# A scan and expert kernel on one core: the first four resident blocks follow chunk 1 instead of chunk 2

## The chip, the cores and the metric

The kernel runs on one core of one Trainium2 chip. The metric is the device time of one execution in microseconds, as the median of several runs; lower is better. Matmuls run on TensorE (PE; its weight loads are PEld), activations on ScalarE (ACT), elementwise work on VectorE (DVE), indirect DMAs are issued by GpSimd (POOL), and the other DMAs by SyncE (SP).

## What is computed

The reference is a gated linear recurrence over 4 sequences of 3,648 steps and 256 channels, followed by a two-level mixture of 16 experts in which each of the 14,592 tokens goes to one expert:

```python
log_a = c * sig_r * np.log(np.clip(a_base, 1e-06, 1.0 - 1e-06))[None, None, :]
a_t = np.exp(log_a)
x_gated = np.sqrt(np.maximum(1.0 - a_t * a_t, 1e-06)) * sig_i * x
for t in range(S):
    h = a_t[:, t] * h + x_gated[:, t]
    y[:, t] = h
...
g_idx = np.argmax(x @ w_group, axis=1)           # 4 groups, then 4 experts in the group
h = np.maximum(xg[mask_e] @ w1[g, e], 0.0)       # 256 -> 1024
out[tok_idx] = combined[:, None] * (h @ w2[g, e])  # 1024 -> 256, scaled by the two softmax weights
```

## The kernel before, in words

**Chunks.** The tokens are cut into 16 chunks (`SIZES`, in tiles of 128 tokens): chunk 0 has 4 tiles, chunks 1 to 13 have 8, the last two 4 and 2. A chunk's gates are loaded by SP (`load`, L251; tiles `a`, `i`, `x`), made on ACT (L322 to L342) and combined and scanned on DVE (L346, L350, L359). PE then turns the scanned columns into rows, two tiles at a time, with the router's logits beside them (`rows1`, L366; one such call is a row group here and stands as x4 in the order and as x8 in the trace, since the profiler lists two matmuls for each). ACT copies the rows (L372), DVE picks the experts and counts them (L385 to L443; `cn`, L422, is the count), PE ranks the tokens (`rank`, L448 and L449), and POOL writes each row, 276 floats, to its place in its expert's list in DRAM (`scatter`, L469, one DMA for each tile, to the tensor `y_s`). A list has a head of 384 unused rows (`HEAD`), and after the last list lies a region of 256 rows that is cleared at the start (`clear`, L313).

**Resident blocks.** Experts 0, 4, 8 and 12 (`RES`) have their weights loaded at the start (`load_raw`, L968, eight loads of 1,024 KB into w1h0, w1l0 and so on). After the chunks in `RSTAGES` (chunks 2 and 3), and before any other expert work, the kernel takes one block of up to 128 tokens from each of these four lists. `counts` (L598) sums the lists' lengths on PE; `near` (L690) works out on DVE where each block starts, and masks the rows that were taken already; `rows_block` (L1017, L479) reads 128 rows on SP into tiles `hl` and `xl`; `turn_block` (L1026) turns them on PE, ACT copies them (L1030), then come two halves of the first product (L1037), two relus on ACT (L1042) and two halves of the second product (L1049), and the result is scaled and scattered to the output (L1054, L1057). Here R0 is the first set of four blocks and R1 the second.

**Units.** All other tokens go in units of 256 rows: 8, 9 and 9 of them are planned after chunks 4, 7 and 10 (`STAGES`) and 11 after the last chunk, and 16 tails, one for each expert, finish the lists. The first 12 units run in plain float32 (L982, L992, L1006) with weights in the places of the resident experts' weights, unit 0 in that of R0's and R1's block 0; the others run as three products of split operands (L861). A unit's weights can only be loaded when the block before it in the same place is done.

**The order.** Every engine runs its instructions in the order in which they were written. A planner (`Plan`, L43 to L138) decides it: each piece of work is an `op` with an engine, a cost, a due time, what it follows and which ring buffers it takes; `run` advances a clock for each engine and emits, among the pieces that could start soonest, the one with the earliest due time. R0's and R1's pieces are due at their chunk's time plus constants (`add_blocks`, L1063; a chunk has 16.5 in the planner's clock), so the chunk number in `RSTAGES` moves them all.

```python
bs = [Block(s, k, ck.due + ORES + k * STEPB) for k in range(NR)]
...
ga = op("SP", 0.1, lambda m=m: rows_block(m), ck.due + 20, [rows] + scattered, [bg], dma=P * DW * 4)
...
w = temp(tb, NR)
V.scalar_tensor_tensor(w, own, -float(P), dn, op0=ALU.add, op1=ALU.min)
...
V.tensor_tensor(tb.ri, w[0:1], er[0:1], op=ALU.add)
```

The last lines are from `near`: a block starts at min(length - 128, what is done) rows from the list's start. A list with fewer than 128 rows gives a negative start, in the head.

Of the kernel before, what the change touches and what calls it, by code (L numbers as in the profile page):

```python
# [8 lines left out]
F32 = mybir.dt.float32  # L9
# [35 lines left out]
class Plan:  # L45
# [14 lines left out]
    def op(self, engine, cost, emit, due, after=(), new=(), use=(), dma=0, table=None, soon=0.0, order=()):  # L60
        o = Op(engine, cost, emit, due, new, use, dma, table, soon)
        after = dict.fromkeys(a for a in after if a)
        order = dict.fromkeys(a for a in order if a and a not in after)
        o.wait = len(after) + len(order)
        for b in o.new + o.use:
            b.left += 1
        for a in after:
            a.then.append(o)
        for a in order:
            a.next.append(o)  # L70
        self.ops.append(o)
        return o
# [70 lines left out]
def rglru_moe_kernel(ctx: ExitStack, tc: tile.TileContext, x, r_gate, i_gate, a_param,  # L143
                     w_group, w_expert, w1, w2, out):
    nc = tc.nc
    V, S, G, T, DMA = nc.vector, nc.scalar, nc.gpsimd, nc.tensor, nc.sync

    P, NB = 128, 4
# [3 lines left out]
    NE = 16  # L152
# [3 lines left out]
    DW = D + LW  # L156
# [3 lines left out]
    TS = 256  # L160
    BPE = NTOK // TS + 2
    HEAD = 3 * P
# [1 line left out]
    SIZES = [4] + [8] * 13 + [4, 2]   # L164
    CH = 8

    RES, RSTAGES = (0, 4, 8, 12), (2, 3)
    STAGES = [(4, 8), (7, 9), (10, 9)]
    NATIVE = 12

# [1 line left out]
    PBUFS = dict(q_r=2, q_y=1, q_h=2, q_o=1)  # L172
    NA = sum(n for _, n in STAGES)
    NR = len(RES)
    assert NR == 4 and RSTAGES[-1] < STAGES[0][0]

    NP = NT >> 1
    NPS = 37 - NA
# [15 lines left out]
    const = ctx.enter_context(tc.tile_pool(name="const", bufs=1))  # L194
# [4 lines left out]
    rings, pools = {}, {}  # L199
# [13 lines left out]
    y_s = dram.tile([NBLK * TS, DW], F32, name="y_s")  # L213
# [13 lines left out]
    op = plan.op  # L227
# [77 lines left out]
        V.tensor_scalar(tcs[:, k:k + 1], tcol, float(k * P), None, op0=ALU.add)  # L305


    zero = const.tile([P, DW // 2], F32, name="zero")
    V.memset(zero, 0.0)

    def clear(dst):
        k = dst.shape[0] // P
        return DMA.dma_start(dst.rearrange("(p k) (a c) -> p (k a) c", k=k, a=2),  # L313
                             zero.unsqueeze(1).broadcast_to([P, 2 * k, DW // 2]))

    cleared = op("SP", 0.1, lambda: clear(y_s[NE * BPE * TS:, :]), 8.0, dma=5e5, soon=8)

# [1027 lines left out]
```

## Time and profile before

| What | Value |
|---|---|
| median of 3 runs | 957.08 us (954.96 to 960.32) |
| the profiled execution | 946.03 us |
| its span in the profile | 944.3 us |
| PE busy | 856.5 us, 6,082 matmuls |
| DVE, ACT, POOL busy | 620.2, 590.5, 287.0 us |
| DMA | 215.60 MB, mean 228 GB/s |

The profiled execution is one run, and it is 11 us under the median of the others; 1.7 us of its time lie outside the span. In the rows that follow, a line of a timeline gives the start in us, the time from first to last instruction of a merged piece, the engine, the line and the operation, and in brackets the idle time before it and what ended it. The code's line numbers of before are one lower than those of after from L313 on.

### The profile page before, as it was taken

What the parts mean: (1) busy time and instruction counts of PE and PEld (TensorE: products, weight loads), DVE (VectorE), ACT (ScalarE), POOL (GpSimd) and SP (SyncE); (2) the same over time, 40 slices, a digit from 0 to 9 for tenths busy, and PEclk for the clock granted to TensorE, in tenths of its full rate; (3) what the DMA queues carried; (4) which work ended last, traced back from release to release, by engine and by line L of the source; (5) the groups of instructions that cost most, each with busy time, mean ns of one, the idle gap of its engine ahead of it and who ended that gap; (6) DMA issues with size and microseconds to landing.
All of it is one profiled execution on the core that took longest, in us unless ns stands there. A gap on an engine that the chain in (4) does not pass through costs nothing. (4 is left out here: it accounts for less than half of the span.)

```text
span 944.3 us, 18467 instructions
## 1 busy us (share of the span) xinstructions
PE 856.5 (91%) x6082; PEld 821.6 (87%) x6082; DVE 620.2 (66%) x1304; ACT 590.5 (63%) x881; POOL 287.0 (30%) x290
## 2 busy tenths in 40 slices
PE   1335889999999999999999999999999999999984
PEld 1235879988989888999999999999999999999984
DVE  3779777675775426677777777777766666575761
ACT  9999889876797324555555555555645555454541
POOL 2244456465643653111111111111111312122222
PEclk9656889999999999999999999999999999999997
DMA  8997777889886756567667767777763657454410
GB/s 318 424 375 247 278 254 265 297 308 393 292 315 242 232 197 207 159 223 235 214 225 225 229 222 225 225 243 255 234 209 130 189 165 229 136 167 155 131 42 21
DMA packets 72456, 215.60 MB, mean 228 GB/s; under 512 B 10504, under 2 KB 28432, under 8 KB 68241
## 3 DMA queue, kind: packets, MB, share of 16 engines
q1 hardware_dynamic: 60464, 183.04, 58.1%
q0 software_dynamic: 11872, 31.10, 8.6%
q8 instruction: 59, 0.97, 0.4%
q14 instruction: 61, 0.49, 0.1%
HBM read 182.76 MB, written 33.43 MB: 229 GB/s over the span
## 5 line engine op out<-in xcount | busy, mean ns | idle before, releaser
L953 POOL DMA_INDIRECT out_dram<-o,cl x122 | 131.7, 1079 | 484.2 <-ACT o L945 286.1
L469 POOL DMA_INDIRECT y_s<-wf,pi x114 | 135.0, 1184 | 112.8 <-issue 71.4
L865 ACT ACTIVATE a<-q_h 128x384 fp32r<-128x384 f32 (+1 forms) x128 | 56.4, 447 | 108.5 <-PE q_h L861 92.8
L861 PE MATMUL q_h<-x,w1h 128*128 128x384 f32 (+1 forms) x512 | 116.1, 316 | 7.4 <-DVE i L868 6.8
L868 DVE SCALAR_TENSOR_TENSOR i<-q_h,a 128x384 fp32r<-128x384 f32 (+1 forms) x128 | 61.7, 497 | 85.3 <-ACT a L865 81.2
L865 ACT ACTIVATE hh<-q_h 128x512 fp32r<-128x512 f32 x100 | 60.3, 603 | 91.1 <-PE q_h L861 80.8
L861 PE MATMUL q_h<-xh,w1h 128*128 128x256 f32 x400 | 113.2, 283 | 0.0
L861 PE MATMUL q_h<-xl,w1h 128*128 128x256 f32 x400 | 112.6, 282 | 0.0
L861 PE MATMUL q_h<-xh,w1l 128*128 128x256 f32 x400 | 112.4, 281 | 0.0
L816 DVE TENSOR_TENSOR w1l<-wf,w1h 128x1024 fp32r<-128x1024 f32 x82 | 99.9, 1222 | 11.8 <-ACT w1h L814 9.8
L868 DVE SCALAR_TENSOR_TENSOR hl<-q_h,hh 128x512 fp32r<-128x512 f32 x100 | 68.9, 689 | 54.3 <-ACT hh L865 54.2
L366 PE MATMUL q_y<-yw,a 128*128 128x148 f32 x368 | 63.3, 318 | 41.2 <-DVE a L359 32.7
L366 PEld LDWEIGHTS q_y<-yw,a 128*128 128x128 f32 x368 | 57.5, 211 | 47.8 <-DVE a L359 18.8
L816 DVE TENSOR_TENSOR w2l<-wf,w2h 128x1024 fp32r<-128x1024 f32 x82 | 98.2, 1219 | 0.0
L861 PEld LDWEIGHTS q_h<-x,w1h 128*128 128x128 f32 x512 | 84.2, 188 | 9.0 <-issue 6.3
L814 ACT CAST w1h<-wf 128x1024 fp32r<-128x1024 f32 x82 | 86.9, 1064 | 0.3 <-issue 0.3
L814 ACT CAST w2h<-wf 128x1024 fp32r<-128x1024 f32 x82 | 83.9, 1043 | 0.0
L861 PE MATMUL q_h<-x,w1l 128*128 128x384 f32 (+1 forms) x256 | 79.7, 311 | 0.0
L861 PEld LDWEIGHTS q_h<-xh,w1h 128*128 128x128 f32 x400 | 75.3, 188 | 0.0
L861 PEld LDWEIGHTS q_h<-xh,w1l 128*128 128x128 f32 x400 | 75.3, 188 | 0.0
L861 PEld LDWEIGHTS q_h<-xl,w1h 128*128 128x128 f32 x400 | 75.2, 188 | 0.0
L359 DVE TENSOR_TENSOR_SCAN a<-a,v 128x1024 f32<-128x1024 f32 (+8 forms) x38 | 67.7, 1796 | 0.1
(341 smaller groups left out, 1930.6 us busy)
## 6 DMA issues: line engine op xcount, KB each, us to landing
wf<-in_moe_w_dram SPq DMA_DIRECT2D x164, 512.0 KB, 4.8
a<-in_r_gate_dram SPq DMA_DIRECT2D x26, 512.0 KB, 10.3
i<-in_i_gate_dram SPq DMA_DIRECT2D x26, 512.0 KB, 9.9
x<-in_x_dram SPq DMA_DIRECT2D x26, 512.0 KB, 8.8
g<-y_s SPq DMA_DIRECT2D x37, 276.0 KB, 4.1
w1h<-in_moe_w_dram SPq DMA_DIRECT2D x8, 1024.0 KB, 7.7
w1l<-in_moe_w_dram SPq DMA_DIRECT2D x8, 1024.0 KB, 9.8
w2h<-in_moe_w_dram SPq DMA_DIRECT2D x8, 1024.0 KB, 9.8
```

Of the source, the lines that this page charges most:

```text
L359: V.tensor_tensor_scan(a[:, sl], a[:, sl], v[:, sl], init, ALU.mult, ALU.add)
L366: T.matmul(q[:, k, h * P:h * P + YW], lhsT=ck.t["a", h][:, (2 * i + k) * P:(2 * i + k + 1) * P], rhs=yw[:, h, :], start=h == 0, stop=h == ...
L469: ins = G.indirect_dma_start(out=y_s, out_offset=bass.IndirectOffsetOnAxis(ap=ck.pi[:, k:k + 1], axis=0), in_=ck.t["yo", k // 4][:, k % 4, ...
L814: S.copy(hi[m.b][:, sl], src)
L816: V.tensor_tensor(lo[m.b][:, sl], src, hi[m.b][:, sl].bitcast(F32), op=ALU.subtract)
L861: T.matmul(q, lhsT=w[m.b][:, c, fs], rhs=mv[:, c, :N], start=n == 0, stop=n == 5)
L865: S.activation(hh, q, AF.Relu)
L868: V.scalar_tensor_tensor(hl, q, 0.0, hh.bitcast(F32), op0=ALU.max, op1=ALU.subtract)
L953: ins = G.indirect_dma_start(out=out, out_offset=bass.IndirectOffsetOnAxis(ap=m.col("idx", h), axis=0), in_=m.o[h], in_offset=None, bounds ...
```

## The change

`RSTAGES` becomes (1, 3): R0 follows chunk 1. By the reference's routing of these inputs, the lists of experts 0, 4, 8 and 12 hold 168, 105, 75 and 97 rows after chunk 1, 200, 173, 193 and 208 after chunk 2, and 215, 209, 337 and 263 after chunk 3. So three of R0's four blocks are now partly filled and start 23, 53 and 31 rows ahead of their lists. These rows are masked in `near`, and they are cleared at the start by a second DMA: the last 128 rows of the heads of lists 0, 4, 8 and 12, 512 rows in all. The source of zeros is now a full row of 276 floats in the first buffer of pool `g` instead of half a row in a tile of its own.

```diff
-    RES, RSTAGES = (0, 4, 8, 12), (2, 3)
+    RES, RSTAGES = (0, 4, 8, 12), (1, 3)
...
-    assert NR == 4 and RSTAGES[-1] < STAGES[0][0]
+    assert NR == 4 and RES == tuple(range(0, NE, NE // NR)) and RSTAGES[-1] < STAGES[0][0]
...
-    zero = const.tile([P, DW // 2], F32, name="zero")
+    zero = pools["g"].tile([P, 2, DW], F32, name="g")[:, 0:1, :]
     V.memset(zero, 0.0)
 
-    def clear(dst):
-        k = dst.shape[0] // P
-        return DMA.dma_start(dst.rearrange("(p k) (a c) -> p (k a) c", k=k, a=2),
-                             zero.unsqueeze(1).broadcast_to([P, 2 * k, DW // 2]))
-
-    cleared = op("SP", 0.1, lambda: clear(y_s[NE * BPE * TS:, :]), 8.0, dma=5e5, soon=8)
+    def clear():
+        k = TS // P
+        DMA.dma_start(y_s[NE * BPE * TS:, :].rearrange("(p k) c -> p k c", k=k), zero.broadcast_to([P, k, DW]))
+        heads = y_s[0:NE * BPE * TS, :].rearrange("(e r) c -> r e c", e=NR)[HEAD - P:HEAD]
+        DMA.dma_start(heads, zero.broadcast_to([P, NR, DW]))
+
+    cleared = op("SP", 0.1, clear, 8.0, dma=(2 + NR) * P * DW * 4, soon=8)
```

Apart from the clears, the planner's order changes from chunk 1's routing until just before chunk 13's rank, in the ninth unit; behind that the instructions of all five engines stand in the same order.

**PE, where R0 begins.** Before, the rows from chunk 4's second row group (the first line) to R0's first product (L1037) and on. `hl` and `xl` are R0's rows, `yw,a` the row groups, `cn,tri` the rank of chunk 3.

```order
L366 MATMUL q_o<-yw,a 128x148 x4
L1026 MATMUL q_r<-yw,hl 128x128 x4
L448 LDWEIGHTS tri
L448 MATMUL q_y<-cn,tri 128x16
L449 LDWEIGHTS ones
L449 MATMUL q_y<-cacc,ones 128x16
L366 MATMUL q_o<-yw,a 128x148 x4
L1037 MATMUL q_h<-xh,w1h_174 128x128 x16
```

After, the rows from chunk 3's first row group (the first line) on.

```order
L367 MATMUL q_y<-yw,a 128x148 x4
L367 MATMUL q_o<-yw,a 128x148 x4
L367 MATMUL q_y<-yw,a 128x148 x4
L1027 MATMUL q_r<-yw,hl 128x128 x4
L367 MATMUL q_o<-yw,a 128x148 x4
L1038 MATMUL q_h<-xh,w1h_174 128x128 x16
L367 MATMUL q_y<-yw,a 128x148 x4
L367 MATMUL q_o<-yw,a 128x148 x4
```

R0's first product moved from behind chunk 4's third row group to behind chunk 3's fourth: 14 row groups are ahead of it instead of 17.

**SP, where R0's rows are read.** Before, the loads of chunk 5 (`i`, `x`, `i`, `x`), of chunk 6's `a` and first `i`, and then the first read (L479).

```order
L251 DMA i<-in_i_gate_dram 128x1024 [waits DMAHW2_49,DVE_49]
L251 DMA x<-in_x_dram 128x1024 [waits DMAHW3_49]
L251 DMA i<-in_i_gate_dram 128x1024 [waits DMAHW4_49,DVE_49]
L251 DMA x<-in_x_dram 128x1024 [waits DMAHW5_49]
L251 DMA a<-in_r_gate_dram 128x1024 [waits DMAHW6_49,PE_49]
L251 DMA a<-in_r_gate_dram 128x1024 [waits DMAHW7_49,DVE_49,PE_49]
L251 DMA i<-in_i_gate_dram 128x1024 [waits DMAHW0_49,DVE_49]
L1017 TENSOR_LOAD sm_570 [waits DVE_49]
L1017 ISA x2
L479 ISA
L479 DMA hl<-y_s 128x276 [waits DMAHW1_49,DMASW0_49]
```

After, the read follows chunk 5's `a` and first `i`.

```order
L251 DMA a<-in_r_gate_dram 128x1024 [waits DMAHW1_49,PE_49]
L251 DMA a<-in_r_gate_dram 128x1024 [waits DMAHW2_49,DVE_49,PE_49]
L251 DMA i<-in_i_gate_dram 128x1024 [waits DMAHW3_49,DVE_49]
L1018 TENSOR_LOAD sm_465 [waits DVE_49]
L1018 ISA x2
L480 ISA
L480 DMA hl<-y_s 128x276 [waits DMAHW4_49,DMASW4_49]
```

The four reads moved ahead of chunk 5's other loads and of chunk 6's first three. POOL's scatters take eight semaphores, DMASW0 to DMASW7, in turn, and a chunk's eight scatters (from chunk 1 to 4) take 1 to 7 and then 0; so the first read waited for the eighth scatter of chunk 2, and now waits for its fourth.

**SP, where R1's rows are read.** Before, the first two reads:

```order
L1017 TENSOR_LOAD sm_874 [waits DVE_49]
L1017 ISA x2
L479 ISA
L479 DMA hl<-y_s 128x276 [waits DMAHW0_49,DMASW0_49]
L1017 TENSOR_LOAD sm_874
L1017 ISA x2
L479 ISA
L479 DMA hl<-y_s 128x276 [waits DMAHW1_49]
```

After, the same two:

```order
L1018 TENSOR_LOAD sm_893 [waits DVE_49]
L1018 ISA x2
L480 ISA
L480 DMA hl<-y_s 128x276 [waits DMAHW1_49,DMASW4_49]
L1018 TENSOR_LOAD sm_893
L1018 ISA x2
L480 ISA
L480 DMA hl<-y_s 128x276 [waits DMAHW2_49,DMASW6_49]
```

The first waited for chunk 3's eighth scatter; now the first waits for chunk 4's fourth and the second for its sixth.

## The prediction

> **What bounds the kernel now.** I read the page's table of slices first, for the stage in which an engine is short of work. In it each digit is the busy share of 23.6 us.
>
> ```profile
> PE   1335889999999999999999999999999999999984
> ACT  9999889876797324555555555555645555454541
> ```
>
> PE has little to do in the first six slices and is full from the seventh, about 140 us, until the last two; ACT is full only in the front. The busy times by stage (PE first, then PEld, DVE, ACT, POOL, granted clock, DMA share, GB/s) say the same in numbers:
>
> ```profile
> 20.00:40.00 20.00, 5.79 (x25) 5.37 (x26) 14.04 (x28) 18.71 (x21) 6.33 (x5) 0.57 1.02 423
> 100.00:120.00 20.00, 16.96 (x112) 15.55 (x111) 16.33 (x43) 18.85 (x25) 9.14 (x10) 0.93 0.76 252
> 120.00:140.00 20.00, 17.48 (x109) 15.38 (x109) 13.20 (x47) 16.12 (x20) 10.98 (x12) 0.88 0.71 256
> 180.00:400.00 220.00, 220.00 (x1223) 197.14 (x1222) 126.72 (x410) 134.22 (x201) 106.55 (x113) 1.00 0.74 262
> 400.00:600.00 200.00, 200.00 (x1690) 200.00 (x1689) 145.61 (x220) 117.04 (x185) 32.66 (x34) 1.00 0.71 225
> ```
>
> Then the waits of PE alone, from 140 us to the end (us in total, times, longest):
>
> ```profile
> PE q_h L861 <- DVE i L868: 6.8, 8, 1.4
> PE q_r L837 <- DVE i L868: 1.2, 4, 0.3
> PE q_h L861 <- ACT o L945: 0.6, 1, 0.6
> ```
>
> In 805 us PE waits 8.6 us. So from 140 us on the time is the list of PE's work, and what the kernel can gain lies ahead of that: the sooner PE has taken a given part of its list, the sooner everything ends. Last I read PE's timeline between 79 and 150 us, with R0's turn (L1026), first products (L1037) and second products (L1049), and R1's first product at 145.24:
>
> ```profile
> 79.91 2.34 PE L366 MATMUL q_y<-yw,a 128*128 128x148 f32 x8 [1.01 <-ACT wf L372]
> 82.05 2.01 PE L366 MATMUL q_o<-yw,a 128*128 128x148 f32 x8
> 90.78 0.60 PE L1026 MATMUL q_r<-yw,hl 128*128 128x128 f32 x4
> 97.05 5.54 PE L1037 MATMUL q_h<-xh,w1h 128*128 128x128 f32 x32
> 105.18 1.27 PE L366 MATMUL q_y<-yw,a 128*128 128x148 f32 x8 [1.03 <-ACT wf L372]
> 113.32 0.17 PE L448 MATMUL q_y<-cn,tri 128*128 128x16 bf16 x1
> 116.64 2.60 PE L1049 MATMUL q_o<-w2l,hh 128*128 128x256 f32 x8 [2.01 <-ACT wf L372]
> 131.92 5.20 PE L1049 MATMUL q_o<-w1l,hh 128*128 128x256 f32 x16 [2.52 <-ACT wf L372]
> 145.24 3.73 PE L1037 MATMUL q_h<-xh,w1h 128*128 128x128 f32 x32
> 148.81 1.17 PE L366 MATMUL q_y<-yw,a 128*128 128x148 f32 x8
> 149.82 3.62 PE L1049 MATMUL q_o<-w1l,hh 128*128 128x256 f32 x16
> ```
>
> From 97.05 on PE is nearly dense, with three stalls on ACT's copies (1.03 + 2.01 + 2.52 = 5.6 us).
>
> **When R0 can start.** Chunk 2's fourth and eighth scatter, chunk 4's first and sixth (used further on), and on SP one of chunk 5's loads, R0's first two reads and the load behind the four:
>
> ```profile
> 76.13 0.98 POOL L469 DMA_INDIRECT y_s<-wf,pi  x1 [0.30 <-issue]
> 82.55 1.21 POOL L469 DMA_INDIRECT y_s<-wf,pi  x1 [0.30 <-issue]
> 118.95 2.67 POOL L469 DMA_INDIRECT y_s<-wf,pi  x1 [6.47 <-issue]
> 127.14 0.98 POOL L469 DMA_INDIRECT y_s<-wf,pi  x1 [0.30 <-issue]
> 66.54 0.42 SPq L251 DMA_DIRECT2D x<-in_x_dram  x1
> 85.31 1.95 SPq L479 DMA_DIRECT2D hl<-y_s  x2
> 89.55 0.43 SPq L251 DMA_DIRECT2D x<-in_x_dram  x1
> hl<-y_s SPq DMA_DIRECT2D x4, 138.0 KB, 2.3
> ```
>
> The row at 82.55 is the eighth; the read goes out 85.31 - 82.55 = 2.76 us behind its start. Although R0 now needs only chunk 1's rows, its read waits for chunk 2's fourth scatter, the row at 76.13: 76.13 + 2.76 = 78.9. Two reads are issued in 1.95 us and the second lands 2.3 us later (the last row, KB and median us to landing): 83.2. On PE the turn of these rows now stands behind chunk 3's third row group, which ends at 79.91 + 2.34 = 82.25, so PE waits about 1 us, turns (0.60), does chunk 3's fourth group (2.0, row 82.05) and begins R0's first product at 83.2 + 0.6 + 2.0 = 85.8, where before it was 97.05: 11.2 us sooner.
>
> **What that is worth.** Three row groups that stood ahead of it now stand behind it. They have to be done all the same, at 149.82 - 148.81 = 1.01 us each: 3.0 us. The lead on PE's list is 11.2 - 3.0 = 8.2 us, if the way from there costs what it cost before, its stalls of 5.6 us included. Without those stalls it is 8.2 + 5.6 = 13.8; with twice as many, 2.6. I keep them as they are: ACT is no emptier (18.85 and 16.12 us of 20 in the two stages) and does the same copies and relus, a chunk sooner.
>
> Each stall costs more than itself. Sixteen second products took 5.20 us behind the stall of 2.52, at a granted clock below 1 (0.88 in that stage), and 3.62 us at 149.82: 1.6 us. The Trainium skill, TensorE: Matmul & The Clock Gate, section What's actually happening, has PE's clock fall to half only after an idle window of about 3.4 us; here 2.52 us was enough, so the trace goes further. By the rule these stalls would cost no clock, and twice as many would leave 1.6 us more of the lead than I have by the row.
>
> **The clears.** The added DMA writes 512 rows of 276 floats, 565 KB. In 20 to 40 us the DMA engines are full (share 1.02, 423 GB/s), so it takes up to 565 / 423 = 1.3 us from the loads there. ACT waited for loads thus, in the first 180 us:
>
> ```profile
> ACT a L322 <- DMA a<-in_r_gate_dram: 2.2, 3, 1.1
> L313 SPq DMA_DIRECT2D y_s<-zero x1: 658/658/658, 6.4 to 6.4; - x1
> ```
>
> Three waits, so ACT sometimes feels it; SP needs some 0.66 us more to issue it. Bounds: 0 and 1.3 + 0.66 = 2.0 us; I take 0.7, nearer to 0, as most loads land well before use. A gain is excluded: nothing was taken away. The larger memset on DVE falls in the first 10 us, where DVE mostly waits.
>
> **SP's queue.** R0's reads now hold back chunk 5's `x`, `i`, `x`: these go when the reads are out, at 78.9 + (89.55 - 85.31) = 83.1 instead of 66.54. How long such a load takes to land, and the first and last of the steps in which DVE counts chunk 3:
>
> ```profile
> x<-in_x_dram SPq DMA_DIRECT2D x26, 512.0 KB, 8.8
> 88.47 0.32 DVE L409 SCALAR_TENSOR_TENSOR oh<-d__631,prio 128x160 f32<-128x160 f32 x1
> 92.47 0.17 DVE L422 CAST cn<-inc 128x16 bf16<-128x16 f32 x1
> ```
>
> The `x` lands at 83.1 + 8.8 = 91.9. DVE combines chunk 5's first half ahead of these steps, so they move back from 88.47 to about 92, and the count to 96. PE ranks chunk 3 behind chunk 4's fourth group, at 85.8 + 5.5 + 4 x 2.0 + 0.6 = 99.9. That covers it by 4 us; without the cover each us would be lost on PE.
>
> **R1's rows.** The second read waits for chunk 4's sixth scatter. Chunk 4's rank comes behind R0's second first product: 99.9 + 3.62 + 3.73 = 107.3 (before 113.32). From rank to first scatter it was 118.95 - 113.32 = 5.6, to the sixth 8.2 more: 121.1, read at 123.9, landed at 126.2. PE asks for the second at 107.3 + 2 x 3.62 + 2 x 3.73 + 3 x 1.01 = 125.0 with no stall, 130.6 with the old ones. Cost 0 to 2 us; I take 0.
>
> **Sum.** 8.2 - 0.7 = 7.5 us. The rest of the list is equal: chunk lists change by 84 rows (512 + 424 taken by R0 and R1 before, 405 + 447 after), but by the reference's routing there remain 11 late units and 9 tails of three blocks in both. The trace bears the count out: each of 16 tails issues 32 matmuls of this kind, and 288 of them are 384 wide, 9 tails of 32.
>
> ```profile
> L861 PE MATMUL q_h<-x,w1h 128*128 128x384 f32 x288 | 74.7, 340 | 0.0
> ```
>
> The profiled execution of 946.03 would become 938.5. It lies 11 us under the median of the runs, 957.08; the front has no reason to differ, so I take the 7.5 us off the median: **949.6 us**.
>
> **Rivals.** *The lead is given back (no change, 957).* PE comes sooner to chunk 7's groups and to unit 0's weights:
>
> ```profile
> 145.85 2.39 DVE L359 TENSOR_TENSOR_SCAN a<-a,v 128x640 f32<-128x640 f32 x2
> 166.32 1.17 PE L366 MATMUL q_y<-yw,a 128*128 128x148 f32 x8
> 153.81 0.34 SPq L976 DMA_DIRECT2D w1l<-in_moe_w_dram  x1
> w1l<-in_moe_w_dram SPq DMA_DIRECT2D x8, 1024.0 KB, 9.8
> 179.19 1.89 PE L992 MATMUL q_h<-xh,w1h 128*128 128x256 f32 x8
> ```
>
> Chunk 7's last scan ended 18 us before its first group, and the weights, 9.8 us after 153.81, landed 15.6 us before use; a lead of 8 eats neither, and the weights' place comes free sooner too. A second way: PE is not really full. PEld is busy 197.14 of 220 us between 180 and 400, so 22.9 us might swallow 7.5. The Trainium skill, Perfetto Trace Analysis, section Identifying the Most-Contended Engine, says that weight-load time and not matmul time tells how near PE is to its limit, which would make it 957. Against it stands that no wait before a PE instruction is listed there. I give 0.08 to this and 0.11 to a smaller lead, 0.19 together.
>
> *Slower.* R1's read is in SP's queue and its turn in PE's; if chunk 4's sixth scatter slips, all of PE stands. With the old stalls the second landing has 130.6 - 126.2 = 4.4 us to spare, so each us of delay beyond that is lost: the forecast turns into a loss of 4.8 when chunk 4's rank comes 7.5 + 4.8 + 4.4 = 16.7 us late, at 124. A rank at 128, with chunk 5's late loads and DVE's queue adding up, gives 949.6 + 20.7 - 4.4 = 965.9. For it speaks that SP's, DVE's and PE's queues are chained there; against it, that before, with PE dense, it came at 113.32. 0.07.
>
> *It does not do what it says:* a twelfth late unit, 96 matmuls of the 1,690 in 200 us, is 11.4 us, 961; the count excludes it on these inputs.
>
> **How the numbers follow.** A measurement of this kernel tells 0.5%, 4.8 us, from no change. Faster by more than that: 0.74; within: 0.19; slower: 0.07. The range goes from no stalls and free clears, 957.08 - 13.8 = 943.3, over twice the stalls and the dear clears (2.6 - 2.0 = 0.6 left), to the no-change case, 957.0.
>
> **What would show it.** R0's first product near 85.8 and R1's near 134 (145.24 - 11.2) in PE's timeline; first read of `hl` near 79; stalls before L1049 and L1026 below 6 us in sum; PE's waits from 140 us on still under 10 us; 6,082 matmuls. Wrong if R1's turn waits for DMA, if PE waits after 140 us, or if the front is shifted by the clears.

## The result, and the profile after

| | before | after |
|---|---|---|
| median | 956.26 us (954.31 to 960.32, 8 runs) | 961.45 us (956.65 to 965.67, 8 runs) |
| ratio | 1 | 1.006, 95% interval 1.0036 to 1.0085 |
| the profiled execution | 946.03 us, span 944.3 | 959.93 us, span 958.1 |
| PE busy | 856.5 us, 6,082 matmuls | 858.1 us, 6,082 matmuls |

The change made the kernel 0.6% slower on the chip of these runs. Before's profiled execution is not one of the 8 and lies below all of them. I come back to this, since it turned out to matter: later runs of the same two kernels on three chips, in jobs of their own, gave 944 us for before, and 0.3 to 0.6% less for after.

In the front of after R0's first product came where it was forecast, and chunk 4's rank and R1's first product came sooner. PE's timeline of after (start, duration, engine, line, operation, idle time before and what ended it), with R0's first product, chunk 4's rank, R1's first two turns, R1's first product and unit 0's first product:

```profile
85.80 3.73 PE L1038 MATMUL q_h<-xh,w1h 128*128 128x128 f32 x32
102.42 0.17 PE L449 MATMUL q_y<-cn,tri 128*128 128x16 bf16 x1
121.87 0.44 PE L1027 MATMUL q_r<-yw,hl 128*128 128x128 f32 x2 [2.12 <-DMA hl<-y_s]
124.81 0.69 PE L1027 MATMUL q_r<-yw,hl 128*128 128x128 f32 x2 [1.22 <-DMA hl<-y_s]
131.97 3.73 PE L1038 MATMUL q_h<-xh,w1h 128*128 128x128 f32 x32
170.41 1.89 PE L993 MATMUL q_h<-xh,w1h 128*128 128x256 f32 x8
```

R0 starts at 85.80 (97.05 before), R1 at 131.97 (145.24), unit 0 at 170.41 (179.19). So PE has a lead of 8.8 us when the units begin. Behind that the profile has what before's did not. The stages from 180 us on, in the columns of the prediction (PE, PEld, DVE, ACT, POOL, granted clock, DMA share, GB/s), in after:

```profile
180.00:200.00 20.00, 16.83 (x84) 14.44 (x85) 13.10 (x55) 16.12 (x21) 12.72 (x14) 0.95 0.92 326
200.00:240.00 40.00, 39.05 (x208) 34.82 (x208) 27.91 (x58) 30.25 (x41) 15.58 (x14) 0.98 0.82 311
240.00:300.00 60.00, 52.51 (x271) 45.99 (x270) 36.40 (x107) 38.60 (x54) 30.11 (x31) 0.91 0.85 297
300.00:400.00 100.00, 95.54 (x489) 83.62 (x489) 42.24 (x174) 40.22 (x72) 40.47 (x46) 0.98 0.54 176
400.00:600.00 200.00, 200.00 (x1686) 199.90 (x1685) 146.75 (x221) 119.64 (x187) 34.31 (x34) 1.00 0.71 224
```

PE was full in all of these stages before. Now 220 - 16.83 - 39.05 - 52.51 - 95.54 = 16.1 us of it are idle between 180 and 400 us, and the granted clock is below 1 there. The lead is lost in that stretch, and more than the lead; from 400 us on the stages are again alike. PE's waits of after from 180 us on (total, times, longest):

```profile
PE q_y L367 <- ACT wf L373: 7.5, 1, 7.5
PE q_h L862 <- DVE i L869: 4.0, 5, 1.4
PE q_o L1007 <- ACT hh L999: 3.6, 1, 3.6
PE q_o L1007 <- issue: 3.1, 1, 3.1
```

PE waits for ACT's copies and relus, and once for something that the profile doesn't name ("issue"). The waits for DVE `i` are the old ones of the prediction.

### The profile page after: what moved, and what is told of

It reads as the page before. It is cut to its first block, busy times and chain, and to the rows that moved or that the text cites. A ratio compares the mean times of both kernels' runs of the same rounds, so it can differ in the third digit from the quotient of the medians.

```text
span 958.1 us, 18461 instructions
## 1 busy us (share of the span) xinstructions
PE 858.1 (90%) x6082; PEld 819.3 (86%) x6082; DVE 622.4 (65%) x1304; ACT 589.0 (61%) x881; POOL 284.6 (30%) x290
```

## The experiments

Ratios are to runs of before made beside the run, on the same chip; such a set is called a job. Line numbers are each kernel's own: in the kernels with a written-out list they are 85 or 86 higher than in before, in those with the longer planner's model 6 higher.

**1. The clears alone** (before's blocks after chunks 2 and 3):

```diff
-    RES, RSTAGES = (0, 4, 8, 12), (1, 3)
+    RES, RSTAGES = (0, 4, 8, 12), (2, 3)
```

> The kernel before with the new clears alone (R0 after chunk 2, R1 after chunk 3 as before; the engines' lists are those of before but for 18 rows). Before is 956.3 us, after 961.5. Theory 1 (the lead of some 8 us is had in the front and lost between 180 and 400 us, because the instructions stand in another order there): 955.6 to 958, ratio 0.999 to 1.002. Theory 2 (lead lost in the same stretch, whatever the order, because PE then runs into the chain of the chunks on ACT, POOL and SP): the same. Theory 3 (the clears or what they push out cost it): 961 or more. The profile also shows whether an execution with the order of before has stalls of PE between 180 and 400 us; the one profiled of before had none, at 946.03.

Measured: 945.32 us, before 943.59; 1.0023 (1.0008 to 1.0039). Slower by some 2 us, so theory 3 (5 us) falls. This chip runs before in 944 us, not 956.

**2. A lead made by leaving work out.** Only half of R0's second products are done:

```diff
-        for i in range(4):
+        for i in range(4 if m.s else 2):
```

> The kernel before, with half of R0's second products left out: 16 of 32 matmuls of 128x256, 4 blocks x 1.81 us = 7.2 us of PE's work, out of the time between 105 and 150 us; part of the output is not computed. No instruction on any engine changes its place, so PE has a lead of 7.2 us with the order of before. Theory 1: the lead carries to the end, 949 us, ratio 0.9925. Theory 2: PE only waits more between 180 and 400 us, 954 to 957, ratio 0.998 to 1.001.

Measured: 943.96 us, 1.0007 (0.9989 to 1.0025). None of the 7.2 us arrives. PE's and DVE's timelines of this run, around chunk 6's rank, show where they go:

```profile
173.55 0.18 PE L448 MATMUL q_y<-cn,tri 128*128 128x16 bf16 x1 [3.26 <-DVE cn L422]
173.62 5.39 PE L1049 MATMUL q_o<-w2l,hh 128*128 128x256 f32 x16
179.85 1.89 PE L992 MATMUL q_h<-xh,w1h 128*128 128x256 f32 x8
```

```profile
166.15 0.16 DVE L485 TENSOR_TENSOR cl<-xl,mR 128x2 int32<-128x2 int32 x1 [6.10 <-DMA out_dram<-o,cl]
173.33 0.16 DVE L422 CAST cn<-inc 128x16 bf16<-128x16 f32 x1
```

DVE stands for 6.10 us at the write of `cl` (places and weights of a block's rows, 4 buffers), until a scatter to the output has read an old one. Chunk 6's count is in DVE's list behind that, and PE waits 3.26 us for it. The 16 second products behind the wait take 5.39 us, at a lower clock (0.50 granted between 176 and 178 us). Unit 0 begins at 179.85; in before, without any lead, at 179.19. Theory 1 (the new order alone is at fault) does not explain this: nothing had changed its place. In before's order there is a second chain, of the chunks, that is as late as PE.

**3 and 4. The two halves of the order crossed.** Every op of the planner has the same name in both kernels, so the emission order of one can be replayed in the other. Run 3 has after's order up to 140 us of its plan and before's from there; run 4 before's order up to 152 us and after's from there. The planner's choice is replaced by a table:

```diff
+            for o in sorted((o for ops in todo.values() for o in ops), key=lambda o: o.rank):
+                t = self.start(o)
+                if t is not None:
+                    best = t, o
+                    break
```

> Kernel after with a list written out by hand: the first 140 us of its own plan (R0 early, as in after), from there on the order in which the kernel before has the same steps. Theory 1: the lead is kept, 956.3 - 7.5 = 949 us, ratio 0.990 to 0.994. Theory 2: 956 to 962, ratio 1.000 to 1.006, with stalls of PE between 180 and 400 us of 10 us or more as in after.

> Kernel before with a list written out by hand: the first 152 us of its own plan (R0 late, no new clears), from there on the order in which the kernel after has the same steps. No lead, and the order of after where after lost. Theory 1: the order alone costs what after lost there, 956.3 + 7.5 + 5.2 = 969 us; at least 962, ratio 1.006 to 1.014. Theory 2: no lead, nothing to lose, 956 to 957, ratio 0.999 to 1.002.

Measured: 947.81 us, 1.0045 (1.0028 to 1.0062), and 949.42 us, 1.0065 (1.0044 to 1.0087). Both lose, and both at the seam. In run 3 PE waits 2.56 us at chunk 5's rank and 2.31 us further on; in run 4 3.42 us:

```profile
144.95 0.18 PE L534 MATMUL q_y<-cn,tri 128*128 128x16 bf16 x1 [2.56 <-DVE mA L759]
158.95 3.54 PE L1135 MATMUL q_o<-w2l,hh 128*128 128x256 f32 x8 [2.31 <-ACT hh L1128]
```

```profile
160.69 3.69 PE L1134 MATMUL q_o<-w2l,hh 128*128 128x256 f32 x16 [3.42 <-DVE o L1139]
```

In run 3 the lead is gone at chunk 5's rank already (144.95; 143.21 in before's profile): the steps on DVE that PE now wants early stand in before's place. The pair says that an order belongs to the lead that it was planned with; it doesn't tell theory 1 from theory 2, as each half brings stalls that neither kernel has.

**5. After again**, unchanged, on another chip.

> The kernel after, unchanged, on the chip of the three that follow. It tells whether the stalls of PE between 180 and 400 us (some 16 us in the profiled execution of after) belong to the kernel or to the chip on which that execution ran, where before took 956 us and not 944. Theory 1 (order of the rest): stalls and ratio as before, 1.004 to 1.009. Theory 4 (new: the chunks' own chain, DVE's count and what DVE waits for, is as late as PE, so that a lead of PE ends in a wait at a rank or at unit 0): ratio 1.000 to 1.008, and on a chip with 944 us for before no stalls after 200 us; the lead is gone before that.

Measured: 940.42 us (936.48 to 945.64), before 944.16; 0.9968 (0.9950 to 0.9986). Here after is faster. The same stages in the same kernel:

```profile
180.00:200.00 20.00, 18.85 (x105) 15.99 (x104) 13.54 (x57) 16.78 (x22) 13.01 (x13) 1.00 0.93 318
200.00:240.00 40.00, 40.00 (x215) 35.97 (x214) 30.58 (x71) 34.13 (x44) 17.01 (x19) 1.00 0.83 323
240.00:300.00 60.00, 60.00 (x333) 53.70 (x332) 43.52 (x126) 47.09 (x74) 30.32 (x30) 1.00 0.85 313
300.00:400.00 100.00, 100.00 (x593) 90.78 (x592) 48.39 (x163) 41.65 (x68) 42.11 (x46) 1.00 0.62 207
```

The stalls from 200 to 400 us go with the job of the result, not with the kernel as such. Theory 1 in the form of these expectations, stalls up to 400 us and 1.004 or more, falls with this run. A short stall is left between 180 and 200 us, and run 18 will trace it to the new order after all.

**6, 7 and 8. More buffers for cl**, in after, in before and in the kernel of run 2, every instruction at its place:

```diff
-    BUFS = dict(i=4, x=4, a=8, v=4, wf=6, g=2, xs=2, hs=2, o=3, cl=4)
+    BUFS = dict(i=4, x=4, a=8, v=4, wf=6, g=2, xs=2, hs=2, o=3, cl=8)
```

> The kernel after with every instruction at the place that it has, but 8 buffers in place of 4 for cl, the places and weights of a unit's rows, which DVE writes and POOL's scatters to the output free. Theory 4: DVE no longer waits for scatters to the output (2.7 us in three waits between 130 and 137 us in the profile of after), so after gets up to 3 us faster than after with 4: ratio to before 0.997 to 1.004. Theory 1: as after with 4 buffers, within 0.2%.

> The kernel before with every instruction at its place and 8 buffers for cl. Its PE waits for nothing between 140 and 200 us in the profile, so taking DVE's waits away (1.7 and 1.1 us) brings little by all theories: 0.997 to 1.001.

> Half of R0's second products left out as in the second run (7.2 us of PE's work; part of the output is not computed), and 8 buffers for cl. In the second run DVE waited 3.5 and 6.1 us for scatters to the output before it could write cl, chunk 6's count stood behind that wait, and PE waited 3.3 us for the count. Theory 4: with that wait gone chunk 6's rank comes at about 168 in place of 173.55 us, and 3 to 7 us of the lead reach the end: ratio 0.993 to 0.997. Theory 2 (the chain of the chunks is late for other reasons): 0.999 to 1.002, as in the second run.

Measured: after 938.55 us, 0.9938 (0.9921 to 0.9955); before 943.22 us, 0.9988 (0.9973 to 1.0003); with the omission 939.61 us, 0.9959 (0.9942 to 0.9975). Run 8 against run 2 is the clear one: the same lead gives 0.4% where it gave nothing, and the rows that stood at 173.55 and 179.85 are

```profile
166.60 0.17 PE L534 MATMUL q_y<-cn,tri 128*128 128x16 bf16 x1
171.20 1.89 PE L1078 MATMUL q_h<-xh,w1h 128*128 128x256 f32 x8
```

The rank comes 7 us sooner and without a wait (168 was expected). Theory 4 holds for this chain in before's order. Some 4 of the 7.2 us arrive; where the rest goes was not traced. For after the two intervals, with 4 and with 8 buffers, just touch, so its gain of some 2 us is likely and no more; run 18, with 4 buffers on another chip, has 0.9937 too.

**9 and 10. Before and after once more**, on a third chip.

> The kernel before once more, for a profile beside the next run, on the same chip. Where before takes 943 to 945 us: PE with under 10 us of waits behind 140 us, as in the profile shown. Where it takes 954 us or more, as on the chip of the result: if the chip is what delays, PE of before has some 10 us of waits between 140 and 400 us too.

> The kernel after, on one more chip. The result gave 1.006, the fifth run 0.997. Theory 5 (after is some 0.3 to 0.4% faster where loads and scatters land as in the profile of before, and loses where they land later): 0.995 to 0.999 where before takes 943 to 945 us, 1.003 to 1.009 where it takes 954 or more. Theory 1 (the new order loses by itself) has 1.003 or more on every chip.

Measured: before 945.41 us in its one profiled run; after 939.82 us, before 944.04; 0.9961 (0.9945 to 0.9976). As theory 5 has it for a chip of 944 us.

**11 and 12. Loads sent later.** Theory 5 says that after has less room on SP's queue. Four register loads more stand behind each gather of the first twelve units, in before (11) and after (12):

```diff
+        if m.native:
+            for _ in range(4):
+                m.reg("ri", [ENG.SP], (NBLK - 1) * TS)
```

> The kernel before with every instruction at its place, and behind each of the 12 gathers of the first twelve units four more register loads on SP, some 0.75 us each (a gather at 194.37 and the weights' load behind it at 195.55 in the fifth run lie one such load and the gather's 0.40 apart). So the loads that stand behind a gather on SP go out some 3 us later, 12 times between 140 and 350 us. Theory 5 (after has less room on SP's queue than before): before loses 0 to 3 us, ratio 1.000 to 1.003. Theory 6 (both have as little): 5 us or more, 1.005 or more.

> The same in the kernel after. In it the a load at 179.76 us stands behind a gather that waits for chunk 6's scatters, and ACT waited 1.7 us for it. Theory 5: after loses 8 us or more against after without the delay (0.997 on two chips), ratio to before 1.005 or more, with PE waiting for ACT at unit 0's q_o near 195 us and after it, as in the execution of the result. Theory 6: as much as before loses. If after loses 0 to 3 us, late loads behind the gathers do not explain the result on the first chip.

Measured: 957.58 us, 1.0023 (0.9992 to 1.0055), and 964.85 us, 1.0078 (1.0046 to 1.0110), with before at 956.86. These two fell on a chip like that of the result. After without the delay has 1.006, from the job of the result, so run 12's ratio above 1.005 says nothing by itself. By these ratios the delay of 3.6 us (a gather at 182.97, the load behind it at 186.96 in run 12) costs each kernel about 0.2%. The 8 us that theory 5 had for after did not come, and nothing shows that after loses more than before; the intervals leave room for a few us of difference. So late loads at the gathers are an unlikely reason for what after loses there. Run 11 shows besides that the order of before stalls there too:

```profile
200.00:240.00 40.00, 38.00 (x199) 33.25 (x198) 23.77 (x73) 28.33 (x38) 20.80 (x21) 0.96 0.91 341
240.00:300.00 60.00, 58.10 (x322) 51.86 (x321) 42.92 (x122) 48.42 (x71) 28.93 (x32) 1.00 0.76 280
300.00:400.00 100.00, 94.96 (x496) 83.00 (x495) 39.12 (x168) 35.02 (x65) 41.06 (x46) 1.00 0.55 185
```

That is 2.0 + 1.9 + 5.0 = 8.9 us idle between 200 and 400 us, delay included, where in the profiles of before at 944 to 946 us PE has none. Before without the delay was not profiled on such a chip.

**13, 14, 15 and 16. A planner that knows what a gather waits for.** In the program a gather from `y_s` waits until all scatters that were emitted ahead of it have landed, whichever rows it needs; the planner's model lets it go when its own chunks' scatters have. SP's waits for that between 140 and 400 us (total, times, longest), in run 5:

```profile
SPq L480 <- DMA y_s<-wf,pi: 122.1, 12, 18.3
```

A gather without the wait wasn't tried, as nothing else keeps its read in order with the writes. Runs 13 (after), 14 (after, 8 buffers for `cl`) and 16 (before) add that; run 15 is run 6 again, all on the chip of run 5.

```diff
+        if o.reads:
+            t = max(t, self.landed + self.HOP)
...
             end = self.wire + self.LAG
+            if o.scatters:
+                self.landed = max(self.landed, end)
```

> The kernel after, with one thing more in the planner's model: a gather from y_s goes out only when all scatters that are issued ahead of it have landed, as the waits on SP's queue show (122 us in 12 waits before gathers, 140 to 400 us, in the fifth run). The planner then puts loads ahead of such a gather instead of behind it. Theory 5 (SP's blocked queue is where after loses): on a chip where before takes 944 us 0.993 to 0.996 (after 0.997), on one where it takes 956 us 0.997 to 1.002 (after 1.006). Theory 6 (the queue has nothing to do with it): as after, within 0.2%.

> The same with 8 buffers for cl, known to the planner. Theory 4 and 5 together: 0.990 to 0.994 where before takes 944 us, 0.995 to 1.000 where it takes 956. If cl alone matters: as after with 8 buffers (0.9938 in the sixth run).

> The kernel after with every instruction at its place and 8 buffers for cl, beside the two, as the one known of the four: 0.992 to 0.996 on a chip of 944 us. On one of 956 us: 1.000 to 1.004 if DVE's waits for cl are part of what after loses there, 1.004 to 1.009 if not.

> The kernel before with the same addition to the planner's model. It tells whether what the addition brings has to do with the change at all: theory 5 has 0.998 to 1.001 (before waits on SP as long, but PE comes too late to feel it); if it brings before as much as after, the queue is no part of the explanation.

Measured, with before at 943.93: run 13 935.89 us, 0.9918 (0.9900 to 0.9937); run 14 934.72 us, 0.9908 (0.9889 to 0.9927); run 15 938.54 us, 0.9940 (0.9921 to 0.9960); run 16 943.85 us, 1.0002 (0.9985 to 1.0019). SP's waits for scatters in run 13:

```profile
SPq L486 <- DMA y_s<-wf,pi: 77.7, 8, 14.7
```

SP waits 20.9 us more there at the loads into `wf` (8.4 in run 5), so its waits for scatters fall from 130.5 to 98.6 us in sum. The addition brings before nothing, though its waits before gathers fall too, from 96.8 us in its profile to 68.6 in run 16; and with it the change is worth 8.0 us by the medians, where 7.5 was the forecast. On this chip it makes up what the change alone left behind (run 5: 0.9968, 0.9950 to 0.9986). `cl` adds little to it.

**17 and 18. The best version and after, side by side**, on one more chip.

> The fastest version so far (gathers wait for scatters in the planner's model, 8 buffers for cl) on one more chip, beside after. Theory 5 with 4: 0.989 to 0.993 where before takes 944 us; where it takes 956 us, 0.995 to 1.000, at least 0.6% better than after beside it.

> The kernel after beside it: 0.995 to 0.999 where before takes 944 us, 1.003 to 1.009 where it takes 956 us.

Measured, with before at 944.48: 935.55 us, 0.9909 (0.9891 to 0.9928), and 938.78 us, 0.9937 (0.9919 to 0.9955). The version of run 14, which run 13 equals within the noise, beats both kernels on two chips. No run put it on a chip of the result's kind.

Runs 18 and 13 show the wait on SP's queue from end to end. In after (run 18): chunk 6's first and fourth scatter on POOL, SP's last load before the gather, the gather and what stands behind it; then ACT, then PE:

```profile
172.98 1.17 POOL L470 DMA_INDIRECT y_s<-wf,pi  x1 [0.30 <-issue]
178.06 0.98 POOL L470 DMA_INDIRECT y_s<-wf,pi  x1 [0.30 <-issue]
```

```profile
170.28 0.35 SPq L977 DMA_DIRECT2D w2h<-in_moe_w_dram  x1
182.20 0.40 SPq L480 DMA_DIRECT2D g<-y_s  x1
182.65 1.46 SPq L251 DMA_DIRECT2D a<-in_r_gate_dram  x1
```

```profile
189.37 1.06 ACT L323 ACTIVATE a<-a 128x1024 f32<-128x1024 f32 x1 [3.75 <-DMA a<-in_r_gate_dram]
194.59 2.19 ACT L339 ACTIVATE v<-v,la 128x1024 f32<-128x1024 f32 x2
196.68 0.45 ACT L946 ACTIVATE o<-q_o,cl 128x256 f32<-128x256 f32 x1
```

```profile
197.19 1.99 PE L1007 MATMUL q_o<-w2l,hh 128*128 128x256 f32 x8 [3.12 <-ACT o L946]
```

From 170.28 to 182.20, 11.9 us, SP issues nothing; the gather then goes out while chunk 6's scatters land. The load of `a` behind it goes out at 182.65; ACT waits 3.75 us for it, comes late to the emptying of `q_o` (one buffer), and PE waits 3.12 us for that. In run 13 `a` goes out at 168.91 and `q_o` is emptied at 188.83:

```profile
168.91 0.43 SPq L257 DMA_DIRECT2D a<-in_r_gate_dram  x1
```

```profile
180.96 1.06 ACT L329 ACTIVATE a<-a 128x1024 f32<-128x1024 f32 x1
188.83 0.46 ACT L952 ACTIVATE o<-q_o,cl 128x256 f32<-128x256 f32 x1
```

Its PE has no wait between 140 and 400 us. The planner moved other steps as well, and the waits that are gone, 1.6 us in run 5 and 3.1 in run 18, are less than the 4.5 us between the medians of runs 5 and 13; so this load explains a part of the gain, and the rest was not traced. In before's profile such a load stands behind a gather as well, but one that goes out 12 us sooner, ahead of chunk 6's first scatter, and ACT waits 0.87 us:

```profile
179.34 1.25 POOL L469 DMA_INDIRECT y_s<-wf,pi  x1 [1.74 <-issue]
```

```profile
170.10 0.38 SPq L479 DMA_DIRECT2D g<-y_s  x1
170.53 1.38 SPq L251 DMA_DIRECT2D a<-in_r_gate_dram  x1
176.03 1.06 ACT L322 ACTIVATE a<-a 128x1024 f32<-128x1024 f32 x1 [0.87 <-DMA a<-in_r_gate_dram]
```

So the change did more than move R0: it let the planner put gather and load on the other side of chunk 6's scatters, at a price that it could not see.

## Why the prediction was wrong, point by point

**When R0 can start: right to about 2 us, and exact by luck.** 85.80 was forecast and measured, but two deviations cancel: the first read goes out at 80.62 (78.9 expected), and PE does not wait for it, since the row groups around R0's turn take 1.27 and 1.17 us instead of the 2.34 and 2.01 of before's rows. Other profiles of after have R0's first product at 83.81 (run 5) to 86.34 (run 18). R1's first product comes at 131.97 (134 expected).

**The lead on PE's list: right in size.** 8.2 us were forecast, 7.5 with the clears. 8.8 stand at unit 0 in the result's profile, 8.5 in that of run 18 (170.72) and 11.3 in those of runs 5 and 10 (167.87 and 167.86), and 8.0 us reach the end in run 13. PE's stalls from R0's to R1's first product sum to 5.8 us in after, close to the 5.6 that I kept, but in other places: 4.7 of them are at R1's turns.

**The clears: too small.** 0.7 us was taken and 2.0 was the upper bound; run 1 has 2.2 us (0.8 to 3.7). It begins where I had looked for it, at ACT's loads. The first row is before's, the second run 1's:

```profile
30.15 1.06 ACT L322 ACTIVATE a<-a 128x1024 f32<-128x1024 f32 x1 [1.14 <-DMA a<-in_r_gate_dram]
31.71 1.06 ACT L323 ACTIVATE a<-a 128x1024 f32<-128x1024 f32 x1 [2.88 <-DMA a<-in_r_gate_dram]
```

ACT waits 1.7 us longer for this load, and chunk 1's rank comes at 55.97 us in place of 54.65. The profiles of after have the same wait (2.7 to 2.9 us in the result and in runs 5, 10 and 18), and those of before have 1.1 and 1.4. So the term was of the right kind and too small. Later in run 1 DVE waits 5.42 us to write `cl` and PE 2.58 us at chunk 6's rank:

```profile
175.60 0.18 PE L449 MATMUL q_y<-cn,tri 128*128 128x16 bf16 x1 [2.58 <-DVE cn L423]
168.19 0.16 DVE L486 TENSOR_TENSOR cl<-xl,mR 128x2 int32<-128x2 int32 x1 [5.42 <-DMA out_dram<-o,cl]
```

That the clears cause this second wait was not tested apart; run 2 has it without them.

**"The rest of the list is equal": this is the step that failed.** PE's work is equal; that PE would do it without waits does not follow from a profile in which it arrives late enough for all that it needs. A full PE says that nothing was later than PE, not by how much everything was earlier. I looked for the room at two places only, chunk 7's last scan and unit 0's weights (18 and 15.6 us), and held the lead for safe. In the result's profile PE is idle for 16.1 us between 180 and 400 us, where it had no wait in before's. Runs 2 and 8 show a place with no room at all in before's order, chunk 6's count behind DVE's write of `cl`; runs 13 and 18 one that the new order made, the load of `a` behind a gather. After itself shows only the second: its profiles in runs 5, 10 and 18 have no wait at a rank from 140 us on, and 1.1 to 3.1 us at unit 0's `q_o`. On chips where before takes 944 us after keeps 3.0 to 5.9 us of the lead (0.9968, 0.9961 and 0.9937); that it would be a part is the rival "the lead is given back" in the form of a smaller lead, to which I gave 0.11.

**"I take the 7.5 us off the median": the second failure.** 946.03 and 957.08 were 11 us apart and I let that stand unexplained. The record doesn't say on which chips these two fell, but they fit two kinds: before takes 943.6 to 944.5 us in five jobs on four chips and 956.3 and 956.9 us in the two others. The profile showed a kernel without stalls, and the median was, as far as run 11 tells, of one with them: run 11, delay included, has 8.9 us of idle PE between 200 and 400 us. So the argument was made on an execution of a kind that none of the 8 measured ones was.

**What after loses on the chip of the result is only in part settled.** Its profile has the same wait of 3.1 us at unit 0's `q_o`, with the load of `a` at 183.13 us as its cause, as in run 18. The others, 7.5 and 3.6 us, end with ACT's work, and ACT then waits for what the profile can't name ("remote"):

```profile
274.29 0.62 ACT L373 COPY wf<-q_y 128x552 f32<-128x552 f32 x1 [7.36 <-remote]
274.96 1.35 PE L367 MATMUL q_y<-yw,a 128*128 128x148 f32 x4 [7.50 <-ACT wf L373]
```

After has more idle time than before (16.1 us between 180 and 400 us against the 8.9 of run 11), and 961 against 956 us agrees with that. Why such chips wait there, and why after does so more, stays open; runs 11 and 12 only speak against late loads behind the gathers.

**The rivals.** The slower one, R1's read behind chunk 4's sixth scatter, did not come: chunk 4's rank is at 102.42, ahead of the 107.3 that I expected, so the read was early enough for PE to lose little. R1's turns do wait for their rows, 2.12 and 1.22 us, where I took 0 and allowed 2, and that was a sign that I had named for being wrong; what was lost there was not lost at ACT's copies. A twelfth unit did not appear either (6,082 matmuls). The Trainium skill, Perfetto Trace Analysis, section Identifying the Most-Contended Engine, was weighed as a rule by which PE, with its weight loads at 90%, might swallow the lead; run 13 speaks against that here, since its PE does the same matmuls 8.0 us sooner. On the clock the runs go both ways: a stall of 3.12 us in run 18 is followed by 8 second products in 1.99 us (1.89 without a stall), the granted clock staying at 1.00 in that stage, and one of 2.58 us in run 1 by 16 in 3.70 us. With that the Trainium skill, TensorE: Matmul & The Clock Gate, section What's actually happening, which has the clock fall after an idle window of about 3.4 us, agrees; the 2.52 us of the prediction do not, and the 3.26 us of run 2, where 16 products took 5.39, lie just below it.

## What to carry to other kernels

A lead on the engine that is full is worth only what the chains that feed it have in hand; for each of them (here the count before every rank, and the loads behind every gather) read how long its last step ended before it was used, all along the stretch, and not at two places. When an early step lets a scheduler reorder the rest, look in the new order for what now stands behind a wait in an in-order queue, and give the scheduler's model that wait. And when a profiled execution and the measured median differ by more than the effect, find out why before taking one for the other.

## What the runs showed of the hardware

The time of one kernel goes with the chip, or with something else that stays the same through a job: before has 956.3 and 956.9 us (two jobs) against 943.6 to 944.5 us (five jobs on four chips), 1.3%, and two orders of the same work change places between them, 1.006 on the one kind, 0.994 to 0.997 on the other. The amount of DMA traffic and the rate of its packets don't tell the two apart in the first 60 us (423 and 414 GB/s in 20 to 40 and 40 to 60 us, in after and in run 5). What does is that the profile of such a job lacks records. The first row is after's list of DMA issues, without the median time to landing, the second that of run 5:

```profile
wf<-in_moe_w_dram SPq DMA_DIRECT2D x164, 512.0 KB
```

```profile
wf<-in_moe_w_dram SPq DMA_DIRECT2D x164, 512.0 KB, 5.0
```

The same rows lack it in runs 11 and 12, and in no other run; before's profile of 946.03 us has it. The Trainium skill, NOTIFIC — the notification-queue block, section Overflow: three behaviours, one of which stalls the engine, says that a full queue of such records can be set to drop them or to stall the engine that makes them. That the lost records and the stalls have one cause would fit, but no run here shows it.

One execution of after also differs from the next by the clock that PE is granted in the front, where it has little to do. The first row is of run 5, the second the same row group in run 18:

```profile
56.57 1.27 PE L367 MATMUL q_o<-yw,a 128*128 128x148 f32 x8 [0.67 <-ACT wf L373]
57.20 2.34 PE L367 MATMUL q_o<-yw,a 128*128 128x148 f32 x8 [0.67 <-ACT wf L373]
```

Between 58 and 60 us the granted clock is 1.00 in run 5 and 0.50 in run 18. Chunk 2's rank follows at 66.25 and 68.58 us, and R0 at 83.81 and 86.34. In the profiles with after's front R0's first product comes at 83.8 to 84.4 us where this row group is short (runs 5, 10, 13 and 14), and at 85.5 to 86.3 us where it is long (the result, runs 6, 12, 15, 17 and 18). So some 2 us of a lead read off one profile go with this clock, and not with the change.
